# The order of five attention chunks in the second half of a fused attention and MoE kernel: the 128-row chunk is moved from second place to last

## The chip, the cores and the metric

The kernel runs on one core of one Trainium2 chip. The metric is device time in microseconds (us) of one execution. A core has TensorE (PE, with its weight loads shown apart as PEld), VectorE (DVE), ScalarE (ACT), GpSimd (POOL), and SyncE (SP), whose queue issues all the DMAs of this kernel.

## What is computed

For 4 batches of 8 heads, 576 positions and 64 columns, attention with a relative-position bias is followed by a two-layer feed-forward part with a squared ReLU.

```python
x = (psi_rel / psi_i)[..., None]
bias = np.maximum(x @ w1 + b1, 0.0) @ w2          # 576 x 576 x 8 heads
scores = scale * np.matmul(q, k.transpose(0, 1, 3, 2)) + bias.transpose(2, 0, 1)[None]
scores = scores - np.max(scores, axis=-1, keepdims=True)
attn = np.exp(scores); attn = attn / (np.sum(attn, axis=-1, keepdims=True) + 1e-09)
x = np.matmul(attn, v)        # then (2304 tokens, 512)
h = np.maximum(x @ w_in, 0.0) # 512 -> 2048
out = h * h @ w_out           # 2048 -> 512
```

## The kernel before

The batches are worked on in two pairs, p = 0 and p = 1. The 576 query rows of a pair are cut into five chunks. Chunks 1 to 4 hold 128 rows of each of the two batches, so 256 tokens. Chunk 0 holds the last 64 rows of each batch, packed into one tile of 128 tokens: it is the short one, half of any other. The table `ORDER` (L40) gives for each pair the order of its chunks.

```python
order = [(p, c) for p in range(2) for c in ORDER[p]]
steps = [(p, c, h) for p, c in order for h in range(H)]
```

A step is one head of one chunk; there are 80 of them, and the last 40 belong to the second pair. The main loop does at each step t:

- `qk` (L377 for chunk 0, L383 and L389 for the others): the scores of the step, into the one PSUM tile `sc`.
- `softmax_a`: DVE adds the bias and takes the row maximum (L405, once for each 128 rows), and ACT takes the exponential (L409, L411). With chunk 0 each is done once, with the others twice.
- `softmax_b`: ACT makes the fp16 high part `a` (L123), POOL the low part (L437, L438), and SP transposes it by DMA into `at` (L440).
- `pv` (L470) for the step three earlier (`LAG`): attention times V, 28 matmuls for a chunk of either size.
- After the eighth head of a chunk `finish_x`: DVE scales the 128 or 256 token rows and splits them into two fp16 parts (L499 to L508), and SP transposes these into `xt` (L510). It then adds the chunk's eight MoE units to the queue `moe`.

A MoE unit is one eighth of the hidden layer for one chunk. `g1` is 24 matmuls (L524) with 256 columns, or 128 for chunk 0, into `hp`; then ACT (L530), DVE (L532, L127) and POOL (L534) make the squared ReLU in two parts `g`. `g2` is 12 matmuls of 512 columns (L547), or 6 for chunk 0, and runs two units behind its `g1` (`GLAG`). So a unit of chunk 0 has half of the work of a full unit on every engine. After the eighth unit ACT copies the result (L554) and SP stores it (L557, for chunk 0 two stores by L561).

A step takes one unit from the queue, and a second one when it holds more than 10:

```python
if len(moe) > BACKLOG:
    moe_unit()
softmax_b(p, c, h)
if last < 0 or steps[last][2] != H - 1:
    moe_unit()
```

The queue is first in, first out, so a chunk's units run while the steps of later chunks are worked on: those of the second pair's chunk 0 begin, before the change, in the sixth step of the chunk that follows it. What is still queued when the steps end runs alone. The K and V of the second pair are loaded and split before its first chunk, in the same order of heads for any order of chunks.

Of the kernel before, what the change touches and what calls it, by code (L numbers as in the profile page):

```python
# [36 lines left out]
HID = "122222222211111000"  # L37

W_AT = [3, 2, 2, 2, 2, 2, 2, 2, 2, 2, 2, 2, 2, 2, 2, 1]
ORDER = [[0, 3, 2, 4, 1], [1, 0, 4, 2, 3]]  # L40
LAG, GLAG = 3, 2
BACKLOG = 10
AHEAD = 3
# [6 lines left out]
def tile_attention_moe(  # L50
# [79 lines left out]
    k_t, v_t, q_t, v32 = {}, {}, {}, {}  # L130
    f32c = [(0, c) for c in ORDER[0][:NF]]

# [430 lines left out]

    order = [(p, c) for p in range(2) for c in ORDER[p]]
    steps = [(p, c, h) for p, c in order for h in range(H)]
# [263 lines left out]
```

## Time and profile before

| | |
|---|---|
| time, median of 3 runs | 669.49 us (669.07 to 672.53) |
| the profiled execution: its own time, its span | 673.4 us, 671.7 us |
| PE busy, PEld busy | 618.1 us (92% of the span), 395.1 us |
| DVE, ACT, POOL busy | 409.6, 384.9, 376.4 us |
| mean granted TensorE clock | 0.958 of full speed |

The busy share is a mean over stages with different limits, so the stages are read apart. In the rows further down, "idle before" in brackets is the time that an engine sat idle before an instruction, and what ended it.

### The profile page before, as it was taken

How to read it: one execution, taken by the hardware profiler on the slowest of the kernel's cores; microseconds unless marked ns; L12 is line 12 of the kernel's file. 1: busy time of each engine (PE TensorE's matmuls, PEld its weight loads, DVE VectorE, ACT ScalarE, POOL GpSimd, SP SyncE). 2: the span in 40 equal slices, each digit the busy share in tenths (PEclk: the TensorE clock that was granted, in tenths of full speed). 3: DMA queues.
4: the chain of work that ended last, by engine and by line, in shares of the span. 5: the costliest groups of instructions: out<-in, count | busy, mean ns of one | idle time of the engine just before them, and what ended most of it. 6: DMA issues, size and time to landing. Idle time of an engine off the chain costs nothing.

```text
span 671.7 us, 15521 instructions
## 1 busy us (share of the span) xinstructions
PE 618.1 (92%) x6048; PEld 395.1 (59%) x6048; DVE 409.6 (61%) x809; ACT 384.9 (57%) x855; POOL 376.4 (56%) x391
## 2 busy tenths in 40 slices
PE   5676689899899999999999999999997999999997
PEld 2233356566455556765666766666664776676664
DVE  7787999898854864596676443446467546424111
ACT  5588789577865655645656532556666555521111
POOL 2665569798665455766675543455565554632221
PEclk9577889799999999999999999999997999999999
DMA  6999888576978777889978976557899678451000
GB/s 232 279 276 297 269 241 242 156 230 160 208 137 188 166 167 166 191 170 220 235 153 163 174 142 117 137 94 168 159 185 214 140 131 167 107 103 32 32 1 31
DMA packets 206568, 112.16 MB, mean 167 GB/s; under 512 B 167072, under 2 KB 183456, under 8 KB 206496
## 3 DMA queue, kind: packets, MB, share of 16 engines
q1 hardware_dynamic: 206496, 111.19, 72.3%
q8 instruction: 47, 0.77, 0.5%
q14 instruction: 25, 0.20, 0.1%
HBM read 55.44 MB, written 15.61 MB: 106 GB/s over the span
## 4 chain that ended last, share of the span: by engine, by line
PE 62%; DVE 11%; DMA 11%; ACT 5%; POOL 5%; issue 4%; SPq 0%; DVEq 0%; POOLq 0%; ACTq 0%
PE o L547 22%; PE hp L524 22%; PE pv L470 6%; DMA at<-a 5%; PE sc L389 4%; DVE hg L290 3%; PE bp L317 3%; DMA biasd<-be 2%; POOL a L438 2%; DVE s L405 2%; DMA bt<-biasd 1%; ACT s L411 1%; PE sc L383 1%; DVE ci L211 1%; PE sc L377 1%
## 5 line engine op out<-in xcount | busy, mean ns | idle before, releaser
L524 PE MATMUL hp<-xt,winH 128*128 128x256 f16 (+1 forms) x1280 | 196.0, 263 | 2.6 <-DMA xt<-xh 2.2
L547 PE MATMUL o<-woutH,g 128*128 128x512 f16 x576 | 185.9, 382 | 1.4 <-ACT o L554 0.8
L524 PE MATMUL hp<-xt,winL 128*128 128x256 f16 (+1 forms) x640 | 162.4, 262 | 0.0
L524 PEld LDWEIGHTS <-winH 128*128 128x128 f16 x1280 | 117.1, 98 | 36.1 <-issue 16.0
L547 PEld LDWEIGHTS <-g 128*128 128x128 f16 x864 | 82.8, 98 | 93.2 <-issue 9.1
L532 DVE TENSOR_TENSOR r<-hp,r 128x512 f32<-128x512 f32 (+1 forms) x80 | 50.7, 634 | 135.6 <-ACT r L530 135.5
L438 POOL TENSOR_TENSOR a<-s,a 128x1024 f16<-128x1024 f32 (+1 forms) x64 | 130.2, 2034 | 0.0
L534 POOL TENSOR_TENSOR g<-r,g 128x512 f16<-128x512 f32 (+1 forms) x80 | 86.0, 1075 | 78.5 <-DVE g L127 76.5
L405 DVE CUSTOM_DVE_ANT_0 s<-sc,bt 128x576 f32<-128x576 f32 x144 | 103.5, 751 | 31.7 <-PE sc L389 22.2
L411 ACT ACTIVATE s<-s,nm 128x576 f32<-128x576 f32 x144 | 111.4, 773 | 6.8
L547 PE MATMUL o<-woutL,g 128*128 128x512 f16 x288 | 109.9, 382 | 0.0
L437 POOL TENSOR_TENSOR a<-s,a 128x128 f16<-128x128 f32 (+1 forms) x64 | 28.8, 450 | 138.3 <-ACT a L123 126.3
L409 ACT ACTIVATE nm<-mx,esc 128x1 f32<-128x1 f32 x144 | 41.3, 287 | 108.2 <-DVE mx L405 108.0
L123 ACT ACTIVATE a<-s 128x1152 f16<-128x1152 f32 (+1 forms) x64 | 70.5, 1102 | 50.9 <-DMA at<-a 49.6
L470 PE MATMUL pv<-v,at 128*128 128x64 f16 (+5 forms) x2112 | 96.8, 208 | 1.5 <-DMA at<-a 1.1
L530 ACT ACTIVATE r<-hp 128x512 f32<-128x512 f32 (+1 forms) x80 | 43.1, 539 | 57.0 <-PE hp L524 56.0
L470 PEld LDWEIGHTS <-at 128*128 128x128 f16 (+1 forms) x1792 | 58.0, 100 | 21.1 <-issue 7.7
L290 DVE TENSOR_SCALAR hg<-tab_t,nb 128x528 f32<-128x528 f32 (+17 forms) x96 | 65.4, 729 | 7.1 <-PE bp L317 6.8
L524 PEld LDWEIGHTS <-winL 128*128 128x128 f16 x640 | 62.8, 98 | 6.2 <-issue 0.4
L317 PE MATMUL bp<-hg,w2s 128*32 128x288 f32 (+17 forms) x352 | 49.0, 544 | 7.1 <-ACT hg L287 3.7
L389 PE MATMUL sc<-k,q 64*128 64x512 f16 x384 | 54.7, 390 | 0.0
L127 DVE TENSOR_SCALAR g<-r 128x512 f16<-128x512 f32 (+1 forms) x61 | 37.2, 610 | 2.4
(72 smaller groups left out, 638.4 us busy)
## 6 DMA issues: line engine op xcount, KB each, us to landing
bt<-biasd SPq DMA_DIRECT2D x64, 288.0 KB, 3.2
stg<-w_in SPq DMA_DIRECT2D x16, 512.0 KB, 5.2
stg<-w_out SPq DMA_DIRECT2D x16, 512.0 KB, 4.9
bt<-biasd SPq DMA_DIRECT2D x32, 144.0 KB, 3.5
qst<-qd SPq DMA_DIRECT2D x32, 128.0 KB, 3.4
out<-o SPq DMA_DIRECT2D x16, 256.0 KB, 2.4
v<-vd SPq DMA_DIRECT2D x8, 320.0 KB, 6.2
stg<-vd SPq DMA_DIRECT2D x8, 320.0 KB, 4.0
```

The lines of the kernel that those rows point to most:

```text
L123: nc.scalar.activation(out=out, in_=in_, func=AF.Copy, scale=scale)
L290: nc.vector.tensor_scalar(ht, tab_t[:, 0:dlen(G)], scl[:, n:n + 1], nb1, op0=ALU.mult, op1=ALU.max)
L317: nc.tensor.matmul(out=bp[32 * t:32 * t + 32, 0:d1 - d0], lhsT=w2s, rhs=ts_[t][:, d0:d1], start=True, stop=True, tile_position=(0, 32 * t))
L389: nc.tensor.matmul(out=sc[:, 1024 * b:1024 * b + 512], lhsT=qt[r, qz, qs], rhs=kt[r, z, 64 * b:64 * b + 512], start=(n == 0), stop=(n == 2 ...
L405: nc.vector.tensor_tensor_reduce(s[:, 576 * b:576 * b + 576], sc[:, 960 * sb:960 * sb + 576], bt, inv, -3.0e38, ALU.add, ALU.max, mx[:, b: ...
L411: nc.scalar.activation(out=sl, in_=sl, func=AF.Exp, bias=nm[:, b:b + 1], accum_out=su[:, h, b:b + 1])
L438: nc.gpsimd.tensor_tensor(av[:, :, 640:1152], ev[:, :, 0:512], av[:, :, 0:512], op=ALU.subtract)
L470: nc.tensor.matmul(out=dst, lhsT=lhsT, rhs=vt[r, 5 * b + blk, :] if f32 else vt[:, vz, 5 * b + blk, :], start=(n == 0), stop=(n == nt - 1) ...
L524: nc.tensor.matmul(out=hp[:, f * T:f * T + T].rearrange("p (b t) -> p b t", b=nb), lhsT=wt[:, k, c0:c0 + 128], rhs=xt[:, 0:nb, z * 4 + k, ...
L532: nc.vector.tensor_tensor(rr, hp[:, 0:2 * T], rr, op=ALU.mult)
L534: nc.gpsimd.tensor_tensor(g[:, 1, 0:2 * T], r[:, 0:2 * T], g[:, 0, 0:2 * T], op=ALU.subtract)
L547: nc.tensor.matmul(out=blk["o"][b], lhsT=g[:, z, c0:c0 + 128], rhs=wt[:, 2 * u + f, :], start=(u == 0 and f == 0 and z == 0 and wt is wout ...
```

## The change

One row of the table is changed.

```diff
-ORDER = [[0, 3, 2, 4, 1], [1, 0, 4, 2, 3]]
+ORDER = [[0, 3, 2, 4, 1], [1, 4, 2, 3, 0]]
```

The first 48 steps are the same. Of the last 32, the eight of chunk 0 go from the front to the end, and those of chunks 4, 2 and 3 each move eight places earlier. The number of instructions of the main loop stays the same on every engine. What moves can be seen on ACT, which touches both the softmax and the units.

First, the place at which chunk 0's units begin before the change. The rows are ACT's in two consecutive steps; L411 is a softmax half, L530 the ReLU of a unit, whose last number is 512 for a full unit and 256 for one of chunk 0. Before:

```order
L530 ACTIVATE r<-hp 128x512
L123 ACTIVATE a<-s 128x2x576
L409 ACTIVATE nm<-mx,esc 128x1
L411 ACTIVATE s,sum<-s,nm 128x576
L530 ACTIVATE r<-hp 128x256
L409 ACTIVATE nm<-mx,esc 128x1
L411 ACTIVATE s,sum<-s,nm 128x576
L123 ACTIVATE a<-s 128x2x576
L409 ACTIVATE nm<-mx,esc 128x1
L411 ACTIVATE s,sum<-s,nm 128x576
L530 ACTIVATE r<-hp 128x256
```

The same stretch of ACT's program with the change:

```order
L409 ACTIVATE nm<-mx,esc 128x1
L411 ACTIVATE s,sum<-s,nm 128x576
L409 ACTIVATE nm<-mx,esc 128x1
L411 ACTIVATE s,sum<-s,nm 128x576
L530 ACTIVATE r<-hp 128x512
L123 ACTIVATE a<-s 128x2x576
L409 ACTIVATE nm<-mx,esc 128x1
L411 ACTIVATE s,sum<-s,nm 128x576
L409 ACTIVATE nm<-mx,esc 128x1
L411 ACTIVATE s,sum<-s,nm 128x576
L530 ACTIVATE r<-hp 128x512
```

Before, a step of two softmax halves carries a unit of 256; with the change it carries one of 512, and this holds for all the steps of chunks 4, 2 and 3.

Second, the end of ACT's program, from the row sum of the last chunk (L479) on. Before:

```order
L479 ACTIVATE rd<-sum,eps 128x8
L530 ACTIVATE r<-hp 128x512 x2
L503 ACTIVATE os<-ax 128x2
L530 ACTIVATE r<-hp 128x512 x5
L554 ACTIVATE o<-o_8525,os 128x512
L554 ACTIVATE o<-o_8526,os 128x512
L530 ACTIVATE r<-hp 128x512 x6
L554 ACTIVATE o<-o_9012,os 128x512
L554 ACTIVATE o<-o_9013,os 128x512
```

With the change:

```order
L479 ACTIVATE rd<-sum,eps 128x4
L123 ACTIVATE a<-s 128x576
L530 ACTIVATE r<-hp 128x512 x3
L503 ACTIVATE os<-ax 128x1
L530 ACTIVATE r<-hp 128x512 x3
L530 ACTIVATE r<-hp 128x256 x2
L554 ACTIVATE o<-o_8582,os 128x512
L554 ACTIVATE o<-o_8583,os 128x512
L530 ACTIVATE r<-hp 128x256 x6
L554 ACTIVATE o<-o_9063,os 128x512
```

The eight units of 256 now stand at the very end, behind the full units that were still queued, and the last result is one tile instead of two.

## Rows read from the trace of the kernel before

**Rows 1.** The page: busy time of PE, and its clock in 40 slices.

```profile
PE 618.1 (92%) x6048; PEld 395.1 (59%) x6048; DVE 409.6 (61%) x809; ACT 384.9 (57%) x855; POOL 376.4 (56%) x391
...
PEclk9577889799999999999999999999997999999999
```

**Rows 2.** Busy time by stretch of the span.

```profile
core 0: us, PE busy (x) PEld busy (x) DVE busy (x) ACT busy (x) POOL busy (x), PEclk, DMA share, GB/s
380.00:471.00 91.00, 91.00 (x968) 60.27 (x968) 41.88 (x88) 41.27 (x90) 42.33 (x44) 1.00 0.68 135
471.00:487.00 16.00, 16.00 (x217) 10.52 (x215) 7.39 (x19) 10.93 (x25) 9.16 (x9) 1.00 0.85 167
487.00:520.00 33.00, 27.45 (x359) 17.43 (x356) 23.10 (x50) 21.22 (x49) 19.56 (x19) 0.90 0.97 198
520.00:585.00 65.00, 65.00 (x687) 44.43 (x684) 32.03 (x71) 38.34 (x82) 34.88 (x31) 1.00 0.71 134
...
606.00:668.10 62.10, 62.02 (x416) 40.41 (x414) 16.61 (x31) 8.83 (x15) 12.70 (x11) 1.00 0.07 18
```

**Rows 3.** The chain of work that ended last: start, us, work.

```profile
483.08 1.45 PE hp L524 x24
484.52 1.29 PE o L547 x6
487.56 1.13 PE hp L524 x19
...
529.89 2.73 PE hp L524 x24
532.61 2.59 PE o L547 x12
536.94 2.73 PE hp L524 x24
```

**Rows 4.** PE's timeline, its waits between 487 and 520 us.

```profile
495.19 0.99 PE L470 MATMUL pv<-v,at 128*128 128x64 f16 x28 [0.41 <-DMA at<-a]
...
497.83 0.99 PE L470 MATMUL pv<-v,at 128*128 128x64 f16 x28 [0.73 <-DMA at<-a]
...
506.41 0.33 PE L383 MATMUL sc<-kz,q 128*128 128x128 f16 x3 [0.47 <-DVE mx L405]
...
514.98 0.48 PE L383 MATMUL sc<-kz,q 128*128 128x128 f16 x3 [3.94 <-DVE mx L405]
```

**Rows 5.** DVE's timeline before the longest wait; POOL's beside it.

```profile
510.97 2.60 DVE L508 SCALAR_TENSOR_TENSOR xh<-x,cc,xh 128x512 f16<-128x512 f32 x1
513.50 0.74 DVE L405 CUSTOM_DVE_ANT_0 s<-sc,bt 128x576 f32<-128x576 f32 x1
...
510.46 2.56 POOL L438 TENSOR_TENSOR a<-s,a 128x1024 f16<-128x1024 f32 x1
```

**Rows 6.** All executions of L508: ns min/median/max, first and last start.

```profile
L508 DVE SCALAR_TENSOR_TENSOR xh<-x,cc,xh x18: 737/750/2603, 90.2 to 613.0; 128x512 f16<-128x512 f32 x18
```

**Rows 7.** Busy time by stretch (columns of group 2) around that wait.

```profile
487.00:510.00 23.00, 21.39 (x304) 14.49 (x301) 15.89 (x37) 15.78 (x36) 14.08 (x15) 1.00 0.97 200
...
515.00:520.00 5.00, 5.00 (x27) 2.04 (x27) 2.21 (x7) 4.81 (x12) 2.45 (x3) 0.51 0.97 209
520.00:525.00 5.00, 5.00 (x62) 3.99 (x59) 1.59 (x2) 2.08 (x4) 3.19 (x3) 1.00 0.43 106
```

**Rows 8.** Timeline: ACT's first and POOL's last work of a short unit.

```profile
515.45 0.36 ACT L530 ACTIVATE r<-hp 128x256 f32<-128x256 f32 x1
...
516.67 0.67 POOL L534 TENSOR_TENSOR g<-r,g 128x256 f16<-128x256 f32 x1 [3.65 <-DVE g L127]
```

**Rows 9.** Timeline and stores at the end of the program.

```profile
668.11 0.69 ACT L554 ACTIVATE o<-o,os 128x512 f32<-128x512 f32 x1 [0.18 <-PE o L547]
...
L557 SPq DMA_DIRECT2D out<-o x16: 332/338/563, 261.3 to 668.8; - x16
L561 SPq DMA_DIRECT2D out<-o x4: 545/569/589, 193.2 to 532.5; - x4
```

## The prediction

> **What bounds the kernel now.** The page comes first: PE is busy for 618.1 of 671.7 us, and its clock, low in the first slices, drops once more in the 31st [rows 1]. So the question for a change of order is where PE is not busy at full clock in the last 32 steps, the only part that moves. The busy times by stretch answer it [rows 2]. From 380 to 471 us, and again from 520 to 585 us, PE is busy in every microsecond at clock 1.00, the other engines for less than two thirds of it. The tail from 606 us, where no attention is left, is PE alone as well, 62.02 of 62.10 us. Only the stretch from 487 to 520 us stands out: 27.45 us busy in 33.00, clock 0.90, and DMA at a share of 0.97 against 0.68 and 0.71 in the full stretches.
>
> What differs there is the size of the units [rows 3]. The chain shows a `g1` of 1.45 us and a `g2` of 1.29 us: the units of chunk 0. From one short `g1` to the next it is 4.48 us, so the step's own attention is 4.48 - 1.45 - 1.29 = 1.74 us on PE. With full units the chain shows 2.73 and 2.59 us, and a period of 7.05 us, which leaves 1.73 us: the same attention. So the softmax, the transposes and the loads of a step with two halves have 7.05 us beside a full unit, but only 4.48 us beside a short one. DMA, nearly full from 487 us on, and DVE can't keep that pace.
>
> PE then waits four times [rows 4]: 0.41 and 0.73 us for the transposed `at`, 0.47 and 3.94 us for the row maximum that frees the score tile. The sum is 5.55 us, which is just what is missing in 33.00 - 27.45. The long one is DVE's [rows 5]: `finish_x` of chunk 4 stands in DVE's program ahead of the next softmax half, and its split L508 took 2.60 us, from 510.97 us, after which L405 could begin at 513.50 us. The wait also costs clock [rows 7]. With waits of 1.61 us spread out the clock stays at 1.00 until 510 us, but after the long one, from 515 to 520 us, 0.51 is granted, about the lower level of 1.2 GHz, while PE is busy throughout; then it is back at 1.00. That is 5.00 x (1 - 0.51) = 2.45 us of PE time lost. Together the stretch loses 8.00 us.
>
> **The change, part by part.** Nothing is added or removed; the units and steps are the same, and so is PE's work. Since PE bounds nearly all of this part, only what PE waits can be won or lost.
>
> *The short units leave the steps.* Chunk 4 now follows chunk 1, and all steps of chunks 4, 2 and 3 carry full units. These are the steps of the stretch from 520 to 585 us [rows 2], with its period of 7.05 us and no wait in 65.00 us. So I take the whole 8.00 us away. The bounds: nothing comes back if steps with full units wait elsewhere (no row of the two full stretches shows it), and all of it if they never do.
>
> *The steps of chunk 0 move to the end.* They have half the softmax and a smaller transpose and carry full units, now those of chunks 2 and 3. Before, they lie between 380 and 471 us, where PE never waits [rows 2]. Cost 0; what hides their chain is the full unit of each step, 5.3 us.
>
> *The short units move to the tail.* After the last `pv` PE had ten full units left, and now has three full and eight short ones: 53.2 us before (10 x 5.32), 37.9 us now (3 x 5.32 + 8 x 2.74). This shorter tail is no gain in itself: the 15.3 us of PE work are done earlier, in stretches that were already full. In the tail PE could wait for the chain from `hp` to `g`. For a short unit it takes 1.89 us from ACT's start at 515.45 us to POOL's end at 517.34 us [rows 8]. Between a `g1` and its own `g2` stand two other units, 5.48 us of PE; for the last unit, where no `g1` follows, two short `g2`, 2.58 us [rows 3]. Both are longer, so 0; had the cover been missing, the last chain would cost at most 1.89 us once.
>
> *The last `finish_x`.* Its DVE work and transposes must end before the first short unit. Before, two tiles were made under two full units with PE 62.02 of 62.10 us busy [rows 2]; now one tile under three. Cost 0.
>
> *The end of the program.* The last result is one tile instead of two, so ACT ends no later (its second copy waited 0.18 us), but it is stored in two parts, and a store of this kind takes SP 0.57 us to issue, against 0.34 us [rows 9]. The second part goes out one such issue later: +0.57 us, between 0.23 us (one slow issue in place of a fast one) and 0.80 us (two in place of one).
>
> Sum: -5.55 - 2.45 + 0.57 = -7.43 us. Against the profiled execution's own 673.4 us that is 666.0 us (span 664.3 us). It is 3.9 us above the median of the runs shown, 669.49 us. I carry the difference over unchanged: 669.49 - 7.43 = **662.1 us**.
>
> One term could belong to the one execution: L508. Over its 18 executions the median is 750 ns and the most 2603 ns [rows 6], and the long one lies beside a POOL instruction that itself took 2.56 us, from 510.46 us [rows 5]. Without this overlap DVE would be free 1.85 us sooner, the wait would be 2.09 us, and the clock might stay up. The Trainium skill, GPSIMD Engine Reference, section Specifications, says that GpSimd shares its SBUF interfaces with VectorE and that DVE instructions with two SBUF inputs contend; L508 reads two. The trace agrees (2.60 against 0.75 us). By this rule the overlap comes back in every execution with this timing, which speaks for 662.1 us; if it was chance, the rival below holds.
>
> **The rivals.**
>
> *Most of the loss is of the profiled execution only.* Then the timed runs lose 0.41 + 0.73 + 0.47 + 2.09 = 3.70 us, the gain is 3.70 - 0.57 = 3.1 us, and the time 666.4 us. For it: the profiled execution lies 3.9 us above the median, close to the 1.85 + 2.45 = 4.3 us in question, and one of the three runs (672.53 us) lies 3 us above the two others. Against it: DVE's order puts `finish_x` ahead of the softmax half in every execution, and in a period of 4.48 us POOL's long instruction fills nearly half the time. Chance 0.28.
>
> *The clock falls in the new tail, and the time gets longer.* The tail is then eight short units in a row, 8 x 2.74 = 21.9 us. If they ran at the lower level they would take twice that: 669.49 - 7.43 + 21.9 = 684.0 us. It decides from the point where 7.4 us of them, not quite three units, run at half speed. Against it: from 471 to 487 us short units ran at clock 1.00, and from 487 to 510 us they did so in spite of 1.61 us of waits [rows 2, 7], while in the tail nothing else waits. The Trainium skill, TensorE: Matmul & The Clock Gate, section HAM oscillation, says that small groups of matmuls with waits in between lose the clock again and again; by it the tail would stay fast only as long as the chain of each unit is covered. Chance 0.05.
>
> *The change does nothing that counts.* The long wait appears at another `finish_x`, beside full units. There the cover is 7.05 us a step instead of 4.48 us; the part of 3.94 us above the difference of 2.57 us would be 1.4 us. For a time within 0.5% three such waits with a lost clock would have to be new. No row of the full stretches shows one. About 668 us, chance 0.07.
>
> **How the numbers follow.** My forecast has a chance of 0.58, with its own range of 660.5 to 664.5 us (8.9 to 5.0 us gained: the timed runs may lose a little more or less than the profiled one). The first rival has 0.28, spread from 664.5 to 668.0 us around 666.4 us; the slower one 0.05, no effect 0.07, and 0.02 is left for more than forecast. A change of 0.5%, 3.35 us, is about what a measurement of this kernel can tell from none: faster is below 666.1 us, slower above 672.8 us. Faster takes the forecast, 0.02, and nearly half of the first rival: 0.73. Within 0.5% are the rest of that and the case of no effect: 0.22. Slower: 0.05. The range from 660.5 to 667.3 us holds the forecast and most of the first rival, 8 in 10.
>
> **What would show it.** PE busy in every microsecond from about 380 us to the end; periods of 7.05 us with no short `g1` among the steps of chunks 4, 2 and 3; a granted clock of 1.00 until the last matmul; eight units of 2.74 us back to back at the end; a span near 664.3 us. I am wrong if PE waits in one of the full steps, if the short units in the tail stand apart or run at a lower clock, or if the timed gain is much smaller than the one between the two profiles, which would put the loss down to the one execution.

## The result, and the profile after

| | before | with the change |
|---|---|---|
| time, median of 6 runs | 670.62 us (669.07 to 672.53) | 663.81 us (663.06 to 674.14) |
| ratio, with its 95% interval | | 0.990 (0.988 to 0.992) |

The change saves 6.8 us, 1.0% (5.4 to 8.2 us by the interval). Forecast were 662.1 us, a range of 660.5 to 667.3 us, and 7.4 us saved.

The first profile of the changed kernel fell on an execution in which the clock was low between 80 and 160 us (0.72, against 0.90 before), ahead of all that the change moves, so the rows shown here are those of a second execution, whose own time was 664.1 us and whose span was 662.4 us; the only profile of the order 1, 4, 2, 0, 3 further down is of such an execution too (0.74 there).

Busy time by stretch of the changed kernel, with the columns of [rows 2]:

```profile
380.00:471.00 91.00, 91.00 (x948) 61.01 (x946) 49.57 (x105) 52.09 (x112) 50.15 (x42) 1.00 0.77 155
471.00:487.00 16.00, 16.00 (x182) 10.75 (x180) 6.30 (x15) 10.26 (x20) 8.30 (x8) 1.00 0.71 144
487.00:520.00 33.00, 33.00 (x331) 22.15 (x330) 17.93 (x41) 18.39 (x41) 19.10 (x18) 1.00 0.79 163
520.00:585.00 65.00, 65.00 (x688) 43.88 (x686) 30.99 (x66) 30.23 (x65) 32.60 (x33) 1.00 0.69 133
...
606.00:657.80 51.80, 51.80 (x484) 34.38 (x481) 13.99 (x32) 7.64 (x16) 11.15 (x13) 1.00 0.13 23
```

PE is busy in every microsecond from 380 to 657.8 us, at clock 1.00. The stretch from 487 to 520 us, which had 27.45 us of work and a clock of 0.90 [rows 2], is as full as the others, and its DMA share is down from 0.97 to 0.79. The first profile, apart from its early part, says the same: busy for 287.00 of 287.00 us from 380 to 667 us.

The chain of work that ended last, in the middle and at the end, answers to [rows 3]:

```profile
537.21 2.73 PE hp L524 x24
539.93 2.59 PE o L547 x12
544.26 2.73 PE hp L524 x24
...
639.43 1.34 PE hp L524 x24
640.77 1.29 PE o L547 x6
642.07 1.34 PE hp L524 x24
...
652.61 1.34 PE hp L524 x24
653.95 3.90 PE o L547 x18
```

The period in the steps is 544.26 - 537.21 = 7.05 us, with full units. The short units follow each other in the tail every 642.07 - 639.43 = 2.64 us, which is 1.34 + 1.29 us: none waits. The timeline at the end of the program answers to [rows 9]:

```profile
657.93 0.69 ACT L554 ACTIVATE o<-o,os 128x512 f32<-128x512 f32 x1 [3.50 <-PE o L547]
658.64 1.15 SPq L561 DMA_DIRECT2D out<-o  x2
```

From ACT's last copy to the end of the span it is 662.4 - 657.93 = 4.5 us, against 671.7 - 668.11 = 3.6 us before. The two stores take SP 1.15 us to issue.

The first half of the program takes a different time in each execution: step 44, which is the same in all the kernels here, begins between 341.6 and 353.5 us in the profiles. So it helps to count from its first score matmul, behind which those of 36 more steps follow in every kernel. Before, and with the change:

```profile
344.94 0.33 PE L383 MATMUL sc<-kz,q 128*128 128x128 f16 x3
...
343.50 0.33 PE L383 MATMUL sc<-kz,q 128*128 128x128 f16 x3
```

From this mark to the end of the span it is 671.7 - 344.94 = 326.8 us before and 662.4 - 343.50 = 318.9 us with the change: 7.9 us less. The other 1.4 us between the two spans lie ahead of the mark. The first profile of the changed kernel gives 672.4 - 353.52 = 318.9 us as well.

### The profile page after: what moved, and what is told of

It reads as the page before. It is cut to its first block, busy times and chain, and to the rows that moved or that the text cites. A ratio compares the mean times of both kernels' runs of the same rounds, so it can differ in the third digit from the quotient of the medians.

```text
span 672.4 us, 15527 instructions
## 1 busy us (share of the span) xinstructions
PE 624.7 (93%) x6048; PEld 401.2 (60%) x6048; DVE 411.3 (61%) x809; ACT 386.5 (57%) x855; POOL 376.8 (56%) x391
## 4 chain that ended last, share of the span: by engine, by line
PE 71%; DMA 10%; DVE 9%; POOL 4%; issue 3%; ACT 2%; SPq 0%; DVEq 0%; POOLq 0%; ACTq 0%
PE hp L524 24%; PE o L547 23%; PE pv L470 10%; PE sc L389 5%; PE bp L317 4%; DVE hg L290 3%; DMA at<-a 3%; DMA biasd<-be 2%; POOL a L438 2%; PE tp L423 2%; DMA xt<-xh 1%; PE sc L383 1%; DMA bt<-biasd 1%; DVE s L405 1%; PE sc L377 1%
## 5 line engine op out<-in xcount | busy, mean ns | idle before, releaser
L438 POOL TENSOR_TENSOR a<-s,a 128x1024 f16<-128x1024 f32 (+1 forms) x64 | 129.7, 2027 | 0.0
L411 ACT ACTIVATE s<-s,nm 128x576 f32<-128x576 f32 x144 | 111.4, 773 | 6.8
L470 PE MATMUL pv<-v,at 128*128 128x64 f16 (+5 forms) x2112 | 101.9, 211 | 0.8 <-DVE x L482 0.8
L530 ACT ACTIVATE r<-hp 128x512 f32<-128x512 f32 (+1 forms) x80 | 43.1, 539 | 43.7 <-PE hp L524 43.4
L317 PE MATMUL bp<-hg,w2s 128*32 128x288 f32 (+17 forms) x352 | 50.5, 551 | 10.4 <-ACT hg L287 5.2
L470 PEld LDWEIGHTS pv<-v,at 128*64 128x64 f32 (+3 forms) x320 | 35.8, 213 | 13.8 <-issue 10.0
```

The source lines that it names most:

```text
L317: nc.tensor.matmul(out=bp[32 * t:32 * t + 32, 0:d1 - d0], lhsT=w2s, rhs=ts_[t][:, d0:d1], start=True, stop=True, tile_position=(0, 32 * t))
L411: nc.scalar.activation(out=sl, in_=sl, func=AF.Exp, bias=nm[:, b:b + 1], accum_out=su[:, h, b:b + 1])
L438: nc.gpsimd.tensor_tensor(av[:, :, 640:1152], ev[:, :, 0:512], av[:, :, 0:512], op=ALU.subtract)
L470: nc.tensor.matmul(out=dst, lhsT=lhsT, rhs=vt[r, 5 * b + blk, :] if f32 else vt[:, vz, 5 * b + blk, :], start=(n == 0), stop=(n == nt - 1) ...
```

## Experiments

The theory is the prediction's: short units beside full softmax steps leave PE too little to hide these steps with, `finish_x` comes in between, PE waits and loses its clock; the change takes the short units out of the steps. The rivals: the gain comes from the tail, where the last chunk is now a short one; or the loss was one of the profiled execution. Each ratio below is to runs of the kernel before that were timed in the same set; their medians are 673.5 to 673.6 us. The intervals are 3 to 8 us wide, so the time from step 44 to the end, in the profile of the run, is given beside them.

**The same kernel again, for its profile.**

> The changed kernel once more, unaltered, for a profile whose early part is not disturbed. Theory (short units beside full softmax steps starved PE, and now none stand there): 6.5 to 7.5 us faster than before, 663 to 664.5 us; in the profile PE busy in every microsecond from 380 us to the last matmul, clock 1.00 there, no wait of PE over 1 us after 380 us. Rival (the gain comes from the tail, because the last chunk's own units are short): the same time, but the stretch from 487 to 520 us is no fuller than before, and the tail ends sooner after the last attention matmul than its work of 37.9 us asks for.

0.991 of before (0.987 to 0.9945), 6.1 us, and the rows above. The median, 665.52 us, lies above the 663 to 664.5 us expected, as that of the kernel before does in this set. The part after 380 us is as the theory has it, with no wait of PE at all. What the tail rival says is not so: the stretch from 487 us on has become full, and behind the last attention matmul PE has 657.85 - 615.84 = 42.0 us to the last matmul; the `g1` and `g2` that the chain lists there add up to the same 42.0 us, so the tail is no shorter than its work.

**The kernel before again, for a second profile.**

> The kernel before once more, unaltered, for a second profile of the stretch from 487 to 520 us. If the late softmax of that stretch (DVE's split L508 of 2.60 us beside POOL's low part, a wait of PE of 3.94 us, then half clock) comes back in every execution: waits of 5 to 6 us in sum again, the long one again behind that split, and about 2.4 us of clock lost. If it was chance: L508 at 0.75 us there, waits of 3.5 to 4 us in sum, and the clock stays at 1.00.

The timelines of DVE and POOL, and PE's waits, in that second profile:

```profile
512.60 2.60 DVE L508 SCALAR_TENSOR_TENSOR xh<-x,cc,xh 128x512 f16<-128x512 f32 x1
...
512.09 2.56 POOL L438 TENSOR_TENSOR a<-s,a 128x1024 f16<-128x1024 f32 x1
...
499.87 0.99 PE L470 MATMUL pv<-v,at 128*128 128x64 f16 x28 [1.11 <-DMA at<-a]
516.61 0.48 PE L383 MATMUL sc<-kz,q 128*128 128x128 f16 x3 [3.90 <-DVE mx L405]
```

And the busy time by stretch around it (the column after POOL is the clock):

```profile
487.00:511.00 24.00, 22.65 (x336) 15.55 (x335) 15.70 (x36) 16.69 (x41) 14.81 (x16) 1.00 1.00 203
511.00:516.00 5.00, 1.71 (x33) 1.18 (x31) 4.68 (x6) 0.71 (x3) 3.65 (x3) 0.87 0.93 197
516.00:521.00 5.00, 4.39 (x16) 1.44 (x16) 2.83 (x9) 4.75 (x12) 1.83 (x3) 0.50 0.92 201
```

It is the same event 1.6 us later: L508 at 2.60 us beside POOL's 2.56 us, a wait of 3.90 us (3.94 before, [rows 4]), then a clock of 0.50. So the loss was not one of a single execution. From step 44, at 346.80 us, to the end it is 326.5 us, 0.3 us less than in the first profile: what differs between the two executions lies ahead of the mark. Both profiled executions lie above the median of the timed runs, and whether each of these has the event can't be seen without a trace; their gain of 6.8 us (5.4 to 8.2), where this rival left 3.1 us, speaks for it.

**More PE work in the short units, in both orders.** The 24 hidden-layer matmuls of the eight short units of the second pair are computed twice, the second time over the first; in the kernel before, and in the changed one.

```diff
-        for f in range(2):
+        twice = 2 if (blk["p"], blk["c"]) == (1, 0) else 1
+        for f in [0, 1] * twice:
```

> The order of before, 1, 0, 4, 2, 3; but each of the eight short units of the second pair computes its 24 hidden-layer matmuls twice, the second time over the first, so that the result is the same and PE has 8 x 1.35 = 10.8 us more work, all of it in the starved steps (which grow from 4.48 to 5.8 us). Theory (PE waits there for others): most of the 8 us that it lost there is filled, and the kernel is only 3 to 6 us slower than before. Rival (PE is not starved there; the gain of the change comes from the tail): 10 to 11 us slower.

> The changed order, with the same doubling of the eight short units' hidden-layer matmuls (10.8 us more work on PE, same result). Both theories: the units now stand in a tail where PE is alone and never waits, so the whole 10.8 us is paid: 10 to 11.5 us slower than the changed kernel, 674 to 675.5 us. Against the doubled kernel with the order of before this would be 0 to 3 us faster by the theory (1 us by 3 to 6), and 7 us faster by the rival that has the gain in the tail.

In the order of before 1.0075 of the kernel before (1.003 to 1.012), so 5.0 us slower; in the changed order 1.003 (1.0006 to 1.0055). By the medians the latter is 675.04 - 665.52 = 9.5 us slower than the changed kernel, by the two profiled spans 673.2 - 662.4 = 10.8 us. From step 44 to the end it is 330.6 us in the order of before, 3.9 to 4.1 us more than without the doubling, and 329.6 us in the changed order, 10.7 us more. PE's waits in the first of the two, from its timeline, then one pair of instructions on DVE and POOL, and then the busy time by stretch:

```profile
495.83 0.33 PE L383 MATMUL sc<-kz,q 128*128 128x128 f16 x3 [0.61 <-DVE mx L405]
503.62 0.99 PE L470 MATMUL pv<-v,at 128*128 128x64 f16 x28 [0.88 <-DMA at<-a]
...
509.04 2.42 DVE L508 SCALAR_TENSOR_TENSOR xh<-x,cc,xh 128x512 f16<-128x512 f32 x1
...
508.77 2.14 POOL L438 TENSOR_TENSOR a<-s,a 128x1024 f16<-128x1024 f32 x1
```

```profile
487.00:522.00 35.00, 33.51 (x513) 25.13 (x510) 19.31 (x47) 19.56 (x46) 16.93 (x18) 1.00 0.91 173
```

The same work costs about twice as much in the tail as in the steps. With 10.8 us more for PE, the waits in the steps fall from 5.55 to 1.49 us and the clock stays at 1.00, so 4.06 + 2.45 = 6.5 us of it are filled, and 4.3 us should remain; measured are 5.0 us by the timed runs and 3.9 to 4.1 us from step 44 on. The rival that has the gain in the tail expected 10 to 11 us here, and falls. L508 meets POOL's long instruction here too and takes 2.42 us, but this time it stands behind the two softmax halves of its step, and PE doesn't wait. With the extra work in both kernels the changed order is ahead by 1.0 us from step 44 on, which is what the theory expected; by the medians it is 675.04 against 678.18 us, which the two intervals don't tell apart.

**Chunk 0 third of five.** The order is 1, 4, 0, 2, 3.

```diff
-ORDER = [[0, 3, 2, 4, 1], [1, 0, 4, 2, 3]]
+ORDER = [[0, 3, 2, 4, 1], [1, 4, 0, 2, 3]]
```

> The order of the second pair is 1, 4, 0, 2, 3: chunk 0 is only one place later, and its short units run beside chunk 2's steps instead of chunk 4's. Theory: the same loss at the new place, about 57 us later (eight steps of 7.05 us): waits of PE of 4 to 6 us in sum and a stretch at about half clock, between 540 and 580 us; time as before, 669 to 672 us. Rival (it is the early place that is bad, or each place later gives its share): a third to a half of the gain, 667 to 668.5 us.

0.994 of before (0.9895 to 0.998), a gain of 1.5 to 7.1 us, where the theory as I had put it expected none and the rival a third to a half of the change's. From step 44 to the end the first profile of this order and the two taken later give 320.6, 320.5 and 321.3 us, 5.2 to 6.3 us less than before: two thirds to four fifths of what the change brings, more than either expected. The place is right, 50 us later, but the waits are smaller. DVE's and POOL's timelines there, and PE's waits:

```profile
562.50 0.48 DVE L507 TENSOR_SCALAR xh<-x,cc 128x512 f16<-128x512 f32 x1 [1.52 <-DMA xt<-xh]
563.02 0.75 DVE L508 SCALAR_TENSOR_TENSOR xh<-x,cc,xh 128x512 f16<-128x512 f32 x1
563.69 0.75 DVE L405 CUSTOM_DVE_ANT_0 s<-sc,bt 128x576 f32<-128x576 f32 x1
...
564.03 2.13 POOL L438 TENSOR_TENSOR a<-s,a 128x1024 f16<-128x1024 f32 x1
...
565.19 0.33 PE L383 MATMUL sc<-kz,q 128*128 128x128 f16 x3 [1.37 <-DVE mx L405]
567.82 0.39 PE L524 MATMUL hp<-xt,winH 128*128 128x256 f16 x2 [0.80 <-DMA xt<-xh]
```

L508 ended before POOL's long instruction began, and took 0.75 us; PE waited 1.37 and 0.80 us; from 520 to 585 us the clock was 1.00. To see whether that was chance, the same kernel was profiled twice more.

> The order 1, 4, 0, 2, 3 once more, unaltered, for a second profile. Its first profile showed waits of 2.2 us in sum in the starved stretch, L508 at 0.75 us there and the clock at 1.00, against waits of 5.0 to 5.5 us, L508 at 2.60 us and lost clock in both profiles of the kernel before. If this belongs to the order (the split of q, which stands between the two splits of finish_x before the change, stands elsewhere here): L508 at 0.75 us again and waits of 1.5 to 3 us. If it is chance from execution to execution: in this profile or the next L508 at 2 us or more and a wait of over 3 us.

> The same order a third time, for a third profile: the same two expectations.

It belongs to the order, as far as three profiles can tell. In all three profiles L508 took 0.75 us there, PE waited 2.2, 2.1 and 2.8 us, and the clock stayed. In DVE's program of the kernel before, a split of q (L254) stands between the two splits L507 and L508; in this order none does. But that split isn't needed for the meeting: in the changed kernel L507 and L508 of the same `finish_x`, that of chunk 4, follow each other directly, and L508 meets POOL's instruction all the same:

```profile
463.33 0.69 DVE L507 TENSOR_SCALAR xh<-x,cc 128x512 f16<-128x512 f32 x1 [0.52 <-DMA xt<-xh]
464.06 2.50 DVE L508 SCALAR_TENSOR_TENSOR xh<-x,cc,xh 128x512 f16<-128x512 f32 x1
...
463.70 2.31 POOL L438 TENSOR_TENSOR a<-s,a 128x1024 f16<-128x1024 f32 x1
```

There it costs nothing: beside full units PE hands over the next scores only at 466.66 us, when L508 is done, and PE doesn't wait. So the long wait shows only where both come together, the meeting and a short step. What decides whether the two instructions meet stays open.

**finish_x earlier, in both orders.** In the second pair the second tile of `finish_x` gets a buffer of its own, in a pool that is free by then, so that its splits need not wait for the transpose of the first tile.

```diff
-            xh = xh_p.tile([128, 1024], F16, tag="xh", name="xh")
+            if p and b:
+                xh = hg_p.tile([128, 1152], F32, tag="w", name="xh").bitcast(F16)[:, 0:1024]
+            else:
+                xh = xh_p.tile([128, 1024], F16, tag="xh", name="xh")
```

> The order of before, but in the second pair the second tile of finish_x has a buffer of its own (one that is free by then), so that its two splits no longer wait for the transpose of the first tile and stand before or between the softmax halves of the step before. Nothing else is changed; the short units stay in the steps. Theory (the short step is what starves PE, and finish_x coming late in it makes the long wait and the lost clock): the wait of 3.94 us shrinks to under 2 us and the clock stays, so 3 to 6 us faster than before, 0.991 to 0.996, but not the whole gain of the change. Rival (the short units alone make the loss, whatever DVE does): within 1 us of before. Second rival (the gain has to do with the tail): no change.

> The changed order with the same second buffer for finish_x in the second pair. By both theories PE never waits in that part any more, so nothing is to be won: within 1 us of the changed kernel, 6 to 8 us faster than before. If it is faster than that, finish_x still costs something beside full units.

In the order of before 0.989 (0.9835 to 0.9946), in the changed order 0.986 (0.980 to 0.992). The first, by stretch:

```profile
487.00:520.00 33.00, 30.22 (x415) 21.00 (x413) 20.18 (x50) 22.06 (x52) 18.72 (x19) 1.00 0.98 195
520.00:585.00 65.00, 63.72 (x666) 42.52 (x662) 34.42 (x73) 38.38 (x84) 36.93 (x30) 1.00 0.70 141
```

What the buffer takes away stands in the chain of the kernel before, ahead of the long wait: the transposes, the last of which `finish_x` waits for, take most of the time, and L508 comes at their end.

```profile
488.68 6.46 DMA at<-a
...
499.06 5.72 DMA at<-a
...
506.25 3.09 DMA xt<-xh
...
510.97 2.60 DVE xh L508
```

With the buffer the short units are still there, and DMA is as full as before (0.98), but the long wait has shrunk to 1.02 us and the clock is kept. PE still waits 2.78 us in the first stretch and 1.28 us in the second, there for ACT's copy of a result (L557 of that kernel). That is 4.06 us lost instead of 8.00, a gain of 3.9 us; the timed gain, whose interval is wide (3.6 to 11 us), holds this near its lower end. From step 44 to the end it is 323.3 us, 3.2 to 3.5 us less than before, where the change brings 7.6 to 7.9 us. So a little under half of the loss comes from `finish_x` standing late in a short step, and the rest from the short steps themselves. With the buffer L508 (L511 of that kernel) takes 0.74 us in both tiles of chunk 4, so the late place and the meeting with POOL go together here, and this run can't tell them apart. In the changed order the buffer brings nothing: 318.9 us from step 44 to the end, as without it (the medians, of two sets of runs, are 665.01 and 665.52 us). So no version here beats the changed kernel.

**Chunk 0 last but one.** The order is 1, 4, 2, 0, 3.

```diff
-ORDER = [[0, 3, 2, 4, 1], [1, 0, 4, 2, 3]]
+ORDER = [[0, 3, 2, 4, 1], [1, 4, 2, 0, 3]]
```

> The order of the second pair is 1, 4, 2, 0, 3: chunk 0 last but one. Three of its short units run beside chunk 3's last steps, the others in the tail, where they, and no full units, have to hide the finish_x of chunk 3. Theory (PE waits where short units stand beside or in front of something slower): waits of 2 to 5 us around the last finish_x, and a drop of the clock there; 2 to 6 us slower than the changed kernel, 0.994 to 0.999 of before. Rival (each place later gives its share, because of the tail): three quarters to all of the gain, 0.990 to 0.9925 of before, and no wait at the last finish_x.

0.994 of before (0.990 to 0.999), a gain of 0.7 to 6.7 us. From step 44 to the end it is 324.7 us, only 1.8 to 2.1 us less than before. PE's waits at the end of the steps, from the timeline, and then the stretch behind them (clock 0.66):

```profile
607.86 0.99 PE L470 MATMUL pv<-v,at 128*128 128x64 f16 x28 [0.90 <-DMA at<-a]
...
613.36 0.99 PE L470 MATMUL pv<-v,at 128*128 128x64 f16 x28 [0.82 <-DMA at<-a]
...
629.91 0.38 PE L524 MATMUL hp<-xt,winH 128*128 128x256 f16 x2 [2.67 <-DMA xt<-xh]
```

```profile
630.00:635.00 5.00, 5.00 (x32) 3.84 (x32) 0.00 (x0) 0.55 (x1) 0.00 (x0) 0.66 0.00 0
```

The waits add up to 4.39 us, of which 2.67 us are for the last `finish_x`: here short units, not full ones, have to hide it. With 5.00 x (1 - 0.66) = 1.7 us of clock, 6.1 us are lost, 1.9 us less than the 8.00 us before, which agrees with the time from step 44. So the rival, which expected three quarters of the gain or more and no wait at the last `finish_x`, falls: the fourth place is worse than the third, and to stand late is not what counts. The fifth place is free of loss because there the short units stand beside nothing that they would have to hide.

## Why the prediction was right, point by point

- *What bounded the stretch, and that it would fill.* Right, and shown: the stretch is full in both profiles of the changed kernel, the period of the steps is 7.05 us, and no short unit stands among them.
- *The loss of 8.00 us.* Right, and slightly too small: up to ACT's last copy the changed kernel is 8.5 to 8.7 us shorter from step 44 on, and 0.5 to 0.7 us of this stand in no wait and no clock row; where they come from is open. In the second profile of the kernel before the waits of PE are 1.11 and 3.90 us, and the clock falls to 0.50. The first rival (the loss is mostly of one execution) was wrong, and with it the doubt about L508: the overlap with POOL is there in both profiles of that kernel (2.60 us), as the rule of the Trainium skill, GPSIMD Engine Reference, section Specifications, would have it. Where the order keeps the two apart, L508 takes 0.75 us. What the prediction did not say is that the overlap goes on with the change (2.50 us) and is only hidden there.
- *The tail at full clock.* Right: eight short units, 2.64 us apart, at 1.00. The second rival, that the clock falls there, did not come true. The count of the old tail was wrong, without harm, as no term rests on it: the chain of the kernel before has eleven full units behind the last `pv`, not ten, and the second layer of two earlier units (5.2 us) runs in both tails and was left out. The tail went from 62.5 to 42.0 us.
- *The steps of chunk 0 and the last finish_x cost nothing.* Right; PE does not wait there.
- *The end of the program.* Mis-sized: +0.57 us was forecast, and it is 4.5 - 3.6 = 0.9 us. Both stores stand in SP's queue behind the last copy (1.15 us), where before it was one (0.34 us), so 0.81 us of it is the case that the prediction gave as its upper bound, two slow issues in place of a fast one. With this the sum is 8.00 - 0.9 = 7.1 us, against 6.8 us by the timed runs and 7.6 to 7.9 us from step 44 on.
- *Carrying the sum over to the median.* The difference of the profiled execution to the median, 3.9 us, was carried unchanged. The result is 1.7 us above the 662.1 us that this gave: 1.1 us because the median before is 670.62 us over six runs and not 669.49 us, 0.6 us because the gain is 6.8 us and not 7.4 us. The span came out at 662.4 us and not near 664.3 us; 1.4 us of that lie ahead of step 44 and say nothing about the change.

What was not right was the expectation for the third place, that each starved step costs as much as any other. With chunk 0 in third place the short steps bring waits of 2 to 3 us and no loss of clock. The rest of the 8 us, the long wait and the clock, came where two instructions met inside a short step. Another order can keep them apart, and a full unit can hide their meeting, as in the changed kernel.

## What to carry to other kernels

Where a queue of filler work hides a chain of dependent steps, look at the size of the filler that each step gets, not at its mean: here half-size units beside full steps cost 8.0 us, and the same units at the end, with no step beside them, cost nothing. The work of a stage that is not full can be had cheaply: 10.8 us of extra PE work cost 4 to 5 us there and 9.5 to 10.8 us in the tail, and such a doubling is a simple test of whether an engine is starved. Whether a wait belongs to the order of the instructions or to one execution is told by a second profile, the cheapest experiment that there is. And a profile says more of a small change when it is read from a mark just ahead of the change: from step 44 on, two profiles of one kernel agree within 0.3 us, three of another within 0.8 us, while the timed runs leave several us open.

## What the runs showed of the hardware

I had not expected how closely the overlap of DVE and POOL repeats: L508 took 2603 and 2602 ns in two executions of the kernel before, 2497 and 2492 ns in two of the changed kernel, and 0.75 us, in the short steps, in three of the order with chunk 0 third. The one-input split L127 of a short unit is hit as well: 1.94 us beside L438, where it takes 0.29 us alone in the tail. For PE's clock, a single wait of 3.9 us was followed by about 5 us at half speed in both profiles of the kernel before, and one of 2.67 us, behind two smaller ones, by a stretch of 5 us at 0.66, while waits of 1.0 to 2.0 us left it at 1.00 with chunk 0 third and with the extra buffer. Matmuls of 128 columns, each with its own weight load, run at 1.34 us / 24 = 56 ns apart, nearly as efficient for their columns as those of 256 columns at 2.62 us / 24 = 109 ns.
